# Seven block products for the gate and value projections of a sigmoid-attention and ReGLU kernel

## The chip, the cores and the metric

The kernel runs on one core of a Trainium2 chip. The metric is the device time of one execution in microseconds. The engines of the core work side by side, each through its own queue in order: TensorE (PE; its weight loads are listed apart as PEld), VectorE (DVE), ScalarE (ACT), GpSimd (POOL) and SyncE (SP, which here only issues DMAs). They wait for each other through semaphores.

## The reference

Eight batches of 448 tokens, twelve heads of 64. Sigmoid attention, then a feed-forward layer with a gate; cut to what matters:

```python
scores = np.matmul(q, k.transpose(0, 1, 3, 2)) / np.sqrt(64) - np.log(448)
attn = np.matmul(1.0 / (1.0 + np.exp(-scores)), v)            # 8 x 12 x 448 x 64
x = attn.transpose(0, 2, 1, 3).reshape(3584, 768)
gate = np.maximum(x @ w_gate, 0.0)                            # 3584 x 1536
val = x @ w_val
out = (gate * val) @ w_out                                    # 3584 x 768
```

## The kernel before

**Data.** Everything is cast to 16-bit floats on its way in. The weights `wg`, `wv` and `wo` stay in SBUF. Attention gives x transposed: `xT` is 768 features (six tiles of 128 partitions) by 448 tokens. `hT` is the gated product of two batches ("a group"), 12 feature tiles by 896 tokens.

**The pieces of work on TensorE.** A *score unit* (`qk_unit`, line 292) makes the scores of four heads for one of seven key chunks: four matmuls on quarters of the array that run side by side, into two PSUM banks, from which ACT takes two sigmoids into a tile `PT`. *PV* (`pv`, line 239) multiplies seven such tiles with v for four heads, into two banks, from which DVE scales two tiles of `xT` (`put_xT`, line 174). A *projection* (`gv`, line 304, an "f" below) makes one tile of 128 gate and value features for one batch: six matmuls into one bank for the gate, six into another for the value. ACT takes the relu of the gate (line 318), DVE multiplies it with the value into `hT` (line 327). A *down pair* (`down_pair`, line 413, a "y") makes the output of two token tiles by seven block products in place of eight, with sums of the weights (`weight_sums`, line 385, once) and of the tokens (`token_sums`, line 396) that DVE makes. `down` (line 341) makes the seventh token tile of a group in the plain way.

**Order.** It is written out by hand: engines execute in the order of the program text. The loop at line 562 runs over the batches; a batch has 21 score units in six *bursts* of three or four (`cuts`), PV at the third unit of some bursts (`pv_at`), and after each burst the items that the string `mix[m]` names: "f" takes the next projection from a queue, "y" the next down item. While batch b does its attention, the projections of batch b-1 run. After the loop come the last batch's twelve projections and the last group's down items.

**PSUM.** There are eight banks in two rings of four, given out in turn (`next_ring`, line 71). A projection takes two, a score unit two, PV two. A matmul into a bank waits until the engine that read its last content is done.

**Loads and transposes.** The next batch's q, k and v are loaded from POOL's queue (`load`, `load_v`, lines 98 and 104) after the first burst of a batch, when DVE has copied the present ones out (`dma_transposes`, line 208). SP's queue holds the transposing DMAs that give `qkT` (line 216) and the stores of the output (line 339).

Of the kernel before, what the change touches and what calls it, by code (L numbers as in the profile page):

```python
# [17 lines left out]
def kernel(  # L18
# [36 lines left out]
    xTp = ctx.enter_context(tc.tile_pool(name="xTp", bufs=2 * NPAIR))  # L55
    hTp = ctx.enter_context(tc.tile_pool(name="hTp", bufs=2))
    ysbp = ctx.enter_context(tc.tile_pool(name="ysbp", bufs=4))
    gsbp = ctx.enter_context(tc.tile_pool(name="gsbp", bufs=4))
# [3 lines left out]
    rings = [ctx.enter_context(tc.tile_pool(name="ring0", bufs=4, space=bass.MemoryType.PSUM))]  # L62
# [6 lines left out]
    turn = [0]  # L69

    def next_ring():
        i = turn[0] // 4 % len(rings)
        turn[0] += 1
        return rings[i]

    def bank(name):
        return next_ring().tile([P, 512], FP32, tag="ring", name=name)

    def bank16(name):
        return next_ring().tile([P, 1024], FP16, tag="ring", name=name)  # L80
# [88 lines left out]
    def xT_of(b, pr):  # L169
        if (b, pr) not in xT_tiles:  # L170
            xT_tiles[(b, pr)] = xTp.tile([P, S], FP16, tag="xT", name="xT")
        return xT_tiles[(b, pr)]

    def put_xT(b, pr, q0, qn, src):
        nc.vector.tensor_scalar(  # L175
            out=xT_of(b, pr)[:, q0 : q0 + qn],
            in0=src,
            scalar1=XSCALE,
            scalar2=None,
            op0=AOP.mult,  # L180
        )
# [78 lines left out]
    class FirstSlot:  # L260
# [6 lines left out]
        def unit(self, u):  # L267
# [8 lines left out]
            i = self.number * 4 + u  # L276
            if i % 12 < 2:
                PT = early.tile([P, 2, 512], FP16, tag=f"PT{i % 12}", name="PT")
            else:
                PT = PTp.tile([P, 2, 512], FP16, tag="PT", name="PT")  # L280
# [11 lines left out]
    def qk_unit(b, g, c):  # L292
        ps = [bank("qk_ps") for _ in range(2)]
        qk(qkT_tiles[(b, g)], c, 0, NCH, lambda hh: ps[hh][:, 0:S])
        PT = PTp.tile([P, 2, 512], FP16, tag="PT", name="PT")
        for hh in range(2):
            sigmoid(PT[:, hh, 0:S], ps[hh][:, 0:S])
        PT_tiles[(b, g, c)] = PT

# [4 lines left out]
    def gv(b, q0, qn, f, act_relu):  # L304
        ps = []
        for nm, wt in (("g_ps", wg), ("v_ps", wv)):
            ps.append(bank(nm))
            for dc in range(NDC):
# [3 lines left out]
                    xT_tiles[(b, dc)][:, q0 : q0 + qn],  # L312
# [28 lines left out]
    def down(g, t):  # L341
        last = (g, t) == (B // 2 - 1, 2 * S // P - 1)
        ysb = ysbp.tile([P, DM], FP32, tag="ysb", name="ysb")
        for nm, m0, m1 in (("ya", 0, 512), ("yb", 512, DM)):
# [9 lines left out]
            if m0 == 0 or not last:  # L354
                nc.vector.tensor_scalar(
                    out=ysb[:, m0:m1], in0=ps[:, 0 : m1 - m0], scalar1=OUT_SCALE, scalar2=None, op0=AOP.mult
                )
                if last:
                    store(g, t, ysb, m0, m1, (nc.sync, nc.sync))
            else:  # L360
                nc.scalar.activation(
                    ysb[:, m0:m1], ps[:, 0 : m1 - m0], AF.Copy, scale=OUT_SCALE
                )
        if last:
            store(g, t, ysb, 512, DM, (nc.sync, nc.scalar))
        else:
            store(g, t, ysb, 0, DM, (nc.sync, nc.sync))
# [5 lines left out]
    HF, HM = NFC // 2, DM // 2  # L373
    late = {}

    def open_late():
        first_sbuf.close()
        pool = ctx.enter_context(tc.tile_pool(name="late", bufs=1))
        late["T"] = pool.tile([P, 4, HF, HM], FP16, tag="T", name="T")
        late["pool"] = pool  # L380

    def sub(o, a, b):
        nc.vector.tensor_tensor(out=o, in0=a, in1=b, op=AOP.subtract)
# [10 lines left out]
    sums = {}  # L394

    def token_sums(g, p, pool=None, tag="S"):
        h = hT_tiles[g]
        if pool is None:
            S3 = late["pool"].tile([P, 3, HF * P], FP16, tag="S", name="S")
        else:  # L400
            S3 = pool.tile([P, NPAIR, NCH * D], FP16, tag=tag, name="S")
            S3 = S3[:].rearrange("p x y -> p (x y)")[:, 0 : 3 * HF * P].rearrange("p (i y) -> p i y", i=3)
        S1, S2, S4 = (S3[:, i, :].rearrange("p (f t) -> p f t", f=HF) for i in range(3))
        t1, t2 = (slice(t * P, (t + 1) * P) for t in (2 * p, 2 * p + 1))
        A11, A12 = h[:, 0:HF, t1], h[:, HF:NFC, t1]
        A21, A22 = h[:, 0:HF, t2], h[:, HF:NFC, t2]
# [4 lines left out]
        sums[(g, p)] = S1, S2, S4, A21  # L411

    def down_pair(g, p, then=None):
        h, T = hT_tiles[g], late["T"]
        S1, S2, S4, S3 = sums.pop((g, p))
        t1, t2 = (slice(t * P, (t + 1) * P) for t in (2 * p, 2 * p + 1))
        y1, y2 = (ysbp.tile([P, DM], FP32, tag="ysb", name="ysb") for _ in range(2))
        lo, hi = slice(0, HM), slice(HM, DM)

        def product(ps, A, W, first=True):  # L420
            for f in range(HF):
                nc.tensor.matmul(  # L422
                    ps[:, 0:HM],
                    A[:, f, :],
                    W[:, f, :],
                    start=(first and f == 0),
                    stop=(f == HF - 1),
                    skip_group_check=True,
                )

        def plus(o, ps, u):
            nc.vector.scalar_tensor_tensor(  # L432
                out=o, in0=ps[:, 0:HM], scalar=OUT_SCALE, in1=u, op0=AOP.mult, op1=AOP.add
            )

        a = bank("y11")
        product(a, h[:, 0:HF, t1], wo[:, 0:HF, lo])
        nc.vector.tensor_scalar(
            out=y1[:, lo], in0=a[:, 0:HM], scalar1=OUT_SCALE, scalar2=None, op0=AOP.mult
        )  # L440
        b = bank("u3")
        product(b, S2, T[:, 1])
        plus(y1[:, hi], b, y1[:, lo])
        c = bank("y12")
        product(c, S1, T[:, 0])
        product(b, S3, T[:, 2], False)
        plus(y2[:, lo], b, y1[:, lo])
        plus(y2[:, hi], c, y2[:, lo])
        d = bank("y21")
        product(d, h[:, HF:NFC, t2], T[:, 3])  # L450
        plus(y2[:, lo], d, y2[:, lo])
        store(g, 2 * p + 1, y2, 0, DM, (nc.sync, nc.sync))
        if then is not None:
            then()
        product(a, h[:, HF:NFC, t1], wo[:, HF:NFC, lo], False)
        nc.scalar.activation(y1[:, lo], a[:, 0:HM], AF.Copy, scale=OUT_SCALE)  # L456
        product(c, S4, wo[:, HF:NFC, hi], False)
        plus(y1[:, hi], c, y1[:, hi])
        store(g, 2 * p, y1, 0, DM, (nc.sync, nc.sync))
# [10 lines left out]

    def push_down(g):
        for p in range(3):
            y_queue.append(lambda p=p: down_pair(g, p))
        y_queue.append(lambda: down(g, 6))
# [64 lines left out]
    def pv_finish(b):  # L539
        pv_group(b, NG - 1)  # L540
        push_gv(b, 0, S, range(NFC))
        if b % 2:
            push_down(b // 2)

    first_psum.close()
    rings.insert(0, ctx.enter_context(tc.tile_pool(name="ring1", bufs=4, space=bass.MemoryType.PSUM)))
    turn[0] = 0
# [12 lines left out]

    ffn_mix("f", [(1, lambda: both(1, 0))])
    for b in range(1, B):
        cuts = (0, 3, 6, 9, 13, 17, 21) if b == 1 else (0, 4, 7, 11, 14, 18, 21)
        pv_at = {3: 0, 5: 1} if b == 1 else {0: -1, 2: 0, 4: 1}
# [9 lines left out]
        elif b == 2:  # L574
            mix = ["ff", "ff", "ff", "ff", "ff", "ff"]
# [79 lines left out]
```

## Time and profile before

| | |
|---|---|
| median of 3 runs | 416.93 us (416.25 to 418.12) |
| the profiled execution, its own time | 417.76 us |
| the span in its profile, first to last instruction | 416.0 us |
| granted TensorE clock, mean over the span | 0.998 |
| matmuls of gate and value on 448 tokens | 504 + 504, busy 109.6 + 109.0 us |
| score matmuls, PV matmuls on 448 tokens | 588 and 588, busy 39.8 and 32.2 us |
| sigmoids of 448 columns on ACT | 294, busy 133.2 us |
| relu of the gate on ACT, 448 columns | 84, mean 571 ns |
| products into hT on DVE, 448 columns | 84, mean 620 ns |
| xT from PSUM on DVE, 448 columns | 42, busy 24.3 us |
| DMA issues on POOL | busy 49 us, most of it before 70 us |

In the rows of a profile that follow, a row of the timeline has start and length in microseconds, engine, line, operation, what it writes and reads, how many instructions are merged, and in brackets the idle time before it with what ended it. A row of the chain has start, length and what the end of the program depended on there. A row of the groups has busy time and mean of one in nanoseconds. Matmuls are pipelined: the length of a group of six holds the delay of the last one through the array, so the time from one group's start to the next one's is what TensorE pays.

### The profile page before, as it was taken

The numbers are of one execution on the slowest core, as the hardware profiler recorded it, in microseconds if no ns is written. First come the engines' busy times: TensorE is split into PE (matmuls) and PEld (weight loads), VectorE is DVE, ScalarE is ACT, GpSimd is POOL, SyncE is SP. The second block draws the span as 40 slices with busy tenths as digits, with TensorE's granted clock in tenths as the row PEclk, the third lists the DMA queues.
The fourth block names the chain that finished last, engine by engine and source line by source line (L and its number), as shares of the span: only waits on it lengthen the run. The fifth ranks groups of instructions, "written<-read, shape, count | busy, mean of one in ns | idle before, by whom it ended". The sixth has DMA issues, their size and how long they took to land.

```text
span 416.0 us, 8578 instructions
## 1 busy us (share of the span) xinstructions
PE 406.9 (98%) x3596; PEld 225.9 (54%) x3596; DVE 183.9 (44%) x361; ACT 206.2 (50%) x436; POOL 49.4 (12%) x72
## 2 busy tenths in 40 slices
PE   8999999998999999999999999999999999999996
PEld 3678675554455555555455555454445455455563
DVE  2453344232956554533355443443353442522572
ACT  5856767675653434636564346537553634222100
POOL 8642304300300003000030000300000000000000
PEclk9999999999999999999999999999999999999999
DMA  9999976999883356933289053953431221000054
GB/s 152 198 200 204 204 107 104 202 204 164 105 141 77 81 128 105 185 77 71 44 71 230 21 121 84 149 95 79 88 46 28 50 60 41 16 0 2 14 134 119
DMA packets 68792, 43.68 MB, mean 105 GB/s; under 512 B 35857, under 2 KB 65169, under 8 KB 68753
## 3 DMA queue, kind: packets, MB, share of 16 engines
q0 software_dynamic: 30736, 23.33, 37.5%
q1 hardware_dynamic: 37664, 19.47, 24.4%
q8 instruction: 28, 0.46, 0.5%
q10 hardware_dynamic: 352, 0.33, 0.3%
q14 instruction: 12, 0.09, 0.1%
HBM read 47.19 MB, written 11.01 MB: 140 GB/s over the span
## 4 chain that ended last, share of the span: by engine, by line
PE 85%; DMA 13%; POOL 1%; issue 0%; DVE 0%; ACT 0%; POOLq 0%
PE g_ps L309 24%; PE v_ps L309 23%; PE y L422 14%; PE qk_ps L229 7%; PE pv_ps L247 7%; PE u L422 6%; DMA v<-in_v_dram 4%; DMA wg<-in_moe_w_gate_dram 4%; PE ya L347 2%; DMA qkT<-rel 2%; DMA q<-in_q_dram 2%; DMA k<-in_k_dram 1%; PE yb L347 1%; DVE xT L175 0%; PE trt L198 0%
## 5 line engine op out<-in xcount | busy, mean ns | idle before, releaser
L184 ACT ACTIVATE PT<-qk_ps 128x448 f16<-128x448 f32 (+3 forms) x318 | 151.2, 583 | 54.4 <-PE qk_ps L229 53.2
L309 PE MATMUL g_ps<-xT,wg 128*128 128x448 f16 (+2 forms) x648 | 127.4, 332 | 0.2 <-DVE xT L175 0.2
L309 PE MATMUL v_ps<-xT,wv 128*128 128x448 f16 (+2 forms) x648 | 126.8, 332 | 0.0
L327 DVE TENSOR_TENSOR hT<-gate_sb,v_ps 128x448 f16<-128x448 f32 (+2 forms) x108 | 60.7, 568 | 138.6 <-PE v_ps L309 84.7
L318 ACT ACTIVATE gate_sb<-g_ps 128x448 f32<-128x448 f32 (+2 forms) x102 | 53.9, 541 | 73.6 <-PE g_ps L309 73.4
L309 PEld LDWEIGHTS <-wg 128*128 128x128 f16 x648 | 58.5, 98 | 56.0 <-issue 15.0
L309 PEld LDWEIGHTS <-wv 128*128 128x128 f16 x648 | 62.4, 98 | 47.3 <-issue 0.4
L229 PE MATMUL qk_ps<-qkT 64*64 64x448 f16 (+2 forms) x756 | 47.8, 336 | 2.3 <-DMA qkT<-rel 1.5
L175 DVE TENSOR_SCALAR xT<-pv_ps 128x448 f16<-128x448 f32 (+2 forms) x54 | 28.4, 567 | 31.1 <-PE pv_ps L247 31.0
L456 ACT ACTIVATE ysb<-y 128x384 f32<-128x384 f32 x12 | 5.9, 491 | 70.7 <-PE y L422 70.7
L247 PE MATMUL pv_ps<-PT,v 64*64 64x448 f16 (+2 forms) x756 | 37.5, 329 | 1.2 <-DMA v<-in_v_dram 0.6
L422 PEld LDWEIGHTS <-hT 128*128 128x128 f16 x288 | 28.2, 98 | 19.3 <-issue 0.2
L102 POOL DMA_DIRECT2D k<-in_k_dram x14 | 11.0, 783 | 178.8 <-DVE rel L212 172.1
L229 PEld LDWEIGHTS <-qkT 64*64 64x64 f16 x756 | 18.2, 105 | 23.5 <-issue 14.3
L247 PEld LDWEIGHTS <-v 64*64 64x64 f16 x756 | 21.9, 107 | 12.6 <-issue 1.7
L422 PEld LDWEIGHTS <-S 128*128 128x128 f16 x216 | 21.1, 98 | 14.0
L422 PE MATMUL y<-wo,hT 128*128 128x384 f16 x144 | 27.3, 326 | 0.0
L432 DVE SCALAR_TENSOR_TENSOR ysb<-y,ysb 128x384 f32<-128x384 f32 x36 | 20.1, 557 | 12.7 <-PE y L422 10.7
L432 DVE SCALAR_TENSOR_TENSOR ysb<-u,ysb 128x384 f32<-128x384 f32 x24 | 13.4, 558 | 20.5 <-PE u L422 20.2
L422 PE MATMUL u<-T,S 128*128 128x384 f16 x72 | 13.7, 326 | 0.0
L422 PE MATMUL y<-T,S 128*128 128x384 f16 x72 | 13.7, 326 | 0.0
L422 PE MATMUL y<-T,hT 128*128 128x384 f16 x72 | 13.7, 326 | 0.0
(43 smaller groups left out, 184.8 us busy)
## 6 DMA issues: line engine op xcount, KB each, us to landing
out_dram<-ysb SPq DMA_DIRECT2D x54, 192.0 KB, 2.7
k<-in_k_dram POOLq DMA_DIRECT2D x5, 672.0 KB, 11.2
q<-in_q_dram POOLq DMA_DIRECT2D x5, 672.0 KB, 13.6
v<-in_v_dram POOLq DMA_DIRECT2D x8, 336.0 KB, 15.2
v<-in_v_dram POOLq DMA_DIRECT2D x16, 168.0 KB, 14.8
k<-in_k_dram POOLq DMA_DIRECT2D x8, 224.0 KB, 10.8
wo<-in_moe_w_out_dram POOLq DMA_DIRECT2D x1, 1536.0 KB, 19.6
q<-in_q_dram POOLq DMA_DIRECT2D x6, 224.0 KB, 11.7
```

The costliest lines, as they stand in the source:

```text
L102: nc.gpsimd.dma_start(t16[:, xs, cs], rows_of(src, b)[:, xs, cs])
L175: nc.vector.tensor_scalar(out=xT_of(b, pr)[:, q0 : q0 + qn], in0=src, scalar1=XSCALE, scalar2=None, op0=AOP.mult,)
L184: nc.scalar.activation(PT_ap, ps_ap, AF.Sigmoid, bias=sig_bias, scale=qk_scale)
L229: nc.tensor.matmul(out_of(hh)[o : o + 64, :], qkT[rows, c, cols], qkT[rows, NCH + c0 : NCH + c1, cols], start=True, stop=True, tile_positi ...
L247: nc.tensor.matmul(ps[hh][64 * r : 64 * r + 64, 0:qn], v16[rows, 2 * g + hh, c * D : (c + 1) * D], pieces[c][rows, hh, :], start=(c == 0), ...
L309: nc.tensor.matmul(ps[-1][:, 0:qn], wt[:, dc, f * P : (f + 1) * P], xT_tiles[(b, dc)][:, q0 : q0 + qn], start=(dc == 0), stop=(dc == NDC - 1),
L318: nc.scalar.activation(gate_sb[:, 0:qn], ps[0][:, 0:qn], AF.Relu)
L327: nc.vector.tensor_tensor(out=hT_tiles[g][:, f, o : o + qn], in0=gate_sb[:, 0:qn], in1=ps[1][:, 0:qn], op=AOP.mult,)
L347: nc.tensor.matmul(ps[:, 0 : m1 - m0], hT_tiles[g][:, f, t * P : (t + 1) * P], wo[:, f, m0:m1], start=(f == 0), stop=(f == NFC - 1),)
L422: nc.tensor.matmul(ps[:, 0:HM], A[:, f, :], W[:, f, :], start=(first and f == 0), stop=(f == HF - 1), skip_group_check=True,)
L432: nc.vector.scalar_tensor_tensor(out=o, in0=ps[:, 0:HM], scalar=OUT_SCALE, in1=u, op0=AOP.mult, op1=AOP.add)
L456: nc.scalar.activation(y1[:, lo], a[:, 0:HM], AF.Copy, scale=OUT_SCALE)
```

## The change

For the groups of batches 2 and 3, 4 and 5, 6 and 7, gate and value are made for two feature tiles and both batches at once by `gv_pair` (a "w" item). With the two halves of the 768 features, (wg, wv) is a 2 by 2 block matrix and the two batches' xT another; seven block products of three matmuls each, on sums of blocks, stand in for eight. POOL makes the sums of the weights (`gate_sums` once, in place in `wv`; `unit_sums` for each item, one item ahead), DVE those of the two batches (`batch_sums`). Of the six banks that an item takes, one pair `b` collects four products and is read in between: ACT copies, DVE adds. Batches 0 and 1 keep `gv`.

The down pair is rewritten in the same form, with three banks (`b`, `c`, `a`) in place of four. Banks are given out from a list; `later` moves those in use to its end in the order in which they come free. `xT` is one tile a batch (three buffers), `hT` has one buffer in place of two, `gsb` seven in place of four. Batches 3 to 7 have five bursts of 4, 4, 4, 4 and 5 units in place of six; in the last, PV comes after the first unit. Batch 2 takes ten projections in place of twelve and batch 3 the other two. After each burst from the third of batch 3 on, one item of `work` runs: for a group six "w", the single tile "t", and three "y". Before an item the sums of the next are issued (`prepare`); in a down pair that is done before its seventh product. The last group's w, t and y follow the loop, so that the last work is a down pair.

```diff
-    xTp = ctx.enter_context(tc.tile_pool(name="xTp", bufs=2 * NPAIR))
-    hTp = ctx.enter_context(tc.tile_pool(name="hTp", bufs=2))
+    xTp = ctx.enter_context(tc.tile_pool(name="xTp", bufs=3))
+    hTp = ctx.enter_context(tc.tile_pool(name="hTp", bufs=1))
-    gsbp = ctx.enter_context(tc.tile_pool(name="gsbp", bufs=4))
+    gsbp = ctx.enter_context(tc.tile_pool(name="gsbp", bufs=7))
...
+    def bank(name, shape=(P, 512), dtype=FP32):
+        pool, tag = free[0]
+        free.rotate(-1)
+        return pool.tile(list(shape), dtype, tag=tag, name=name)
+    def later(order):
+        keys = [free[i - 8] for i in order]
+        for key in keys:
+            free.remove(key)
+            free.append(key)
...
+    def gate_sums(f0, f1):
+        fs = slice(f0 * P, f1 * P)
+        sub(wv[:, 0:HD, fs], wg[:, 0:HD, fs], wv[:, 0:HD, fs], nc.gpsimd)
+    def unit_sums(g, f):
+        S1, S2, S4 = sums_tile(2 * P)
+        fs = slice(f * P, (f + 2) * P)
+        A11, A12 = wg[:, 0:HD, fs], wg[:, HD:NDC, fs]
+        S3, A22 = wv[:, 0:HD, fs], wv[:, HD:NDC, fs]
+        sub(S2, A22, S3, nc.gpsimd)
+        nc.gpsimd.tensor_tensor(out=S1, in0=S2, in1=A11, op=AOP.add)
+        sub(S4, A12, S2, nc.gpsimd)
+    def batch_sums(g):
...
+        sub(T1, B12, B11)
+        sub(B12, B22, B12)
+        sub(T2, B22, T1)
+        sub(T4, B21, T2)
+    def gv_pair(g, f):
...
+        b, c, a = ([bank(nm) for _ in range(2)] for nm in ("u", "g2", "g1"))
+        later((6, 7, 4, 5, 2, 3))
+        gs = [[gsbp.tile([P, S], FP32, tag="gsb", name="gsb") for _ in range(3)] for _ in range(2)]
...
+        product(b, 0, B11)
+        copy(0, b)
+        product(c, 3, T1)
+        copy(2, c)
+        product(b, 4, T2, False)
+        copy(1, b)
+        product(a, 1, B21)
+        plus(0, a)
+        product(b, 5, T3, False)
+        plus(2, b)
+        product(c, 6, B22, False)
+        plus(1, c)
+        product(b, 2, T4, False)
+        for u in range(2):
+            gated(u, 0, gs[u][0][:], b[u][:, 0:S])
+        for u in range(2):
+            gated(u, S, gs[u][1][:], gs[u][2][:])
...
-        cuts = (0, 3, 6, 9, 13, 17, 21) if b == 1 else (0, 4, 7, 11, 14, 18, 21)
-        pv_at = {3: 0, 5: 1} if b == 1 else {0: -1, 2: 0, 4: 1}
+        if b == 1:
+            cuts, pv_at = (0, 3, 6, 9, 13, 17, 21), {3: (0, 2), 5: (1, 2)}
+        elif b == 2:
+            cuts, pv_at = (0, 4, 7, 11, 14, 18, 21), {0: (-1, 2), 2: (0, 2), 4: (1, 2)}
+        else:
+            cuts, pv_at = (0, 4, 8, 12, 16, 21), {0: (-1, 2), 2: (0, 2), 4: (1, 1)}
...
-            mix = ["ff", "ff", "ff", "ff", "ff", "ff"]
+            mix = ["ff", "ff", "f", "ff", "f", "ff"]
         elif b == 3:
-            mix = ["fff", "fff", "fy", "fy", "fy", "fy"]
+            mix = ["f", "f", "", "", ""]
             open_late()
...
-            ffn_mix(mix[m], hooks.get(m, ()))
+            if mix[m]:
+                ffn_mix(mix[m], hooks.get(m, ()))
+            elif b > 2:
+                next_work()
     pv_finish(B - 1)
-    last = B // 2 - 1
-    token_sums(last, 0)
-    ffn_mix("f" * NFC)
...
+    push_group(B // 2 - 1)
+    while work:
+        next_work()
```

The helpers of `gv_pair`: `product` runs one block product for both feature tiles (two times three matmuls of 448 columns), `copy` is two ACT copies out of PSUM, `plus` two DVE additions of PSUM onto such a copy, `gated` a DVE operation max(gate, 0) x value into `hT`; for the second batch both its inputs lie in SBUF. The new down pair runs, in this order, a product into `b`, one into `c`, one onto `b`, one into `a`, one onto `b`, one onto `c` and one onto `b`, each read by DVE or ACT before the next onto the same bank. DMAs stay as many, except that the last output tile's store is issued in four parts instead of two, and two of the last stores come from ACT's queue.

## The prediction

> **What bounds the kernel now.** I read the page first (engine shares, the chain that ended last), then the chain in order of time, then the timeline of one burst in the middle and of the start of batch 3.
>
> ```profile
> PE 406.9 (98%) x3596; PEld 225.9 (54%) x3596; DVE 183.9 (44%) x361; ACT 206.2 (50%) x436; POOL 49.4 (12%) x72
> PE 85%; DMA 13%; POOL 1%; issue 0%; DVE 0%; ACT 0%; POOLq 0%
> ```
>
> The chain is TensorE for 85% of the span; its DMA part lies at the start and at one place near 92 us. From 104 us on TensorE never waits more than some tenths. So an item's cost is its matmuls' issue time, read from the chain: six of 448 columns 1.136 us (a "product" below), 24 of 384 columns 3.90.
>
> ```profile
> 363.82 1.14 PE v_ps L309 x6
> 364.96 1.14 PE g_ps L309 x6
> 391.56 3.90 PE y L422 x24
> ```
>
> One burst of the present kernel: two score units, PV, two units, then projections.
>
> ```profile
> 206.82 0.57 PE L229 MATMUL qk_ps<-qkT 64*64 64x448 f16 x8
> 207.22 1.49 PE L247 MATMUL pv_ps<-PT,v 64*64 64x448 f16 x28
> 207.25 3.60 ACT L184 ACTIVATE PT<-qk_ps 128x448 f16<-128x448 f32 x8 [0.91 <-PE qk_ps L229]
> 208.75 1.16 DVE L175 TENSOR_SCALAR xT<-pv_ps 128x448 f16<-128x448 f32 x2 [1.13 <-PE pv_ps L247]
> 209.03 1.31 PE L309 MATMUL g_ps<-xT,wg 128*128 128x448 f16 x6
> 210.66 0.62 ACT L318 ACTIVATE gate_sb<-g_ps 128x448 f32<-128x448 f32 x1
> ```
>
> Two units take 0.40 us of TensorE, PV 1.33. The first sigmoid starts 0.43 after the first score matmul; eight take 3.41 until ACT starts its next operation (207.25 to 210.66), 0.43 each. The relu of g_ps is thus 0.4 us late here already, and nobody minds: the next projection has other banks.
>
> The start of batch 3:
>
> ```profile
> 92.37 9.96 DMA qkT<-rel
> 102.38 0.57 PE L229 MATMUL qk_ps<-qkT 64*64 64x448 f16 x8 [1.50 <-DMA qkT<-rel]
> 105.98 0.55 DVE L383 TENSOR_TENSOR T<-wo 128x768 f16<-128x768 f16 x1
> 109.98 1.14 DVE L327 TENSOR_TENSOR hT<-gate_sb,v_ps 128x448 f16<-128x448 f32 x2
> ```
>
> TensorE waits 1.5 us for the transposed q and k, and eight weight sums hold DVE from 105.98 to 109.98, while the products of the first projection are left in PSUM.
>
> **The change part by part. Removed.** Gate and value for a feature tile of two batches take 7 products of 3 matmuls instead of 8: 756 matmuls for 864, 108 fewer at 0.1893 us: -20.4. Bursts of batches 3 to 7 fall from 30 to 25. A change from projections to scores and back costs 0.32 (212.44 + 1.136 = 213.58 to the next g_ps at 214.37 is 0.79, less 0.57 for three units, plus the first product's 1.24 for 1.14): -1.6. The down products keep their 42 matmuls a pair. Together -22.0.
>
> **Batch 3 starts no earlier.** Batch 2 gives two projections (4.54) to batch 3, so TensorE is ready at 100.8 - 4.5 = 96.3. The transpose is issued one projection earlier (90.1), but it landed only when the loads of k, q, wo and v, issued by 76.9 as before, had drained: DMA still moves 205 GB/s in 94:96. If it lands at 102.3 as now, the wait grows by 4.5; if landing follows its issue, by 2.3. I take 4.5, since the loads do not move.
>
> **Weight sums uncovered.** Three projections followed them in the first burst of batch 3, now one. Its multiply still comes behind eight sums, 7.6 us after the batch's start, and ends at 8.2. The fourth score unit of the next burst needs that bank and is ready at 5.2: +3.1 (2 to 4).
>
> **Two banks for three products.** The pair item holds six banks; its third product adds onto the first, so it waits for two ACT copies of it, and these stand behind the burst's sigmoids. In a burst without PV: copies start at 0.43 + 3.41 = 3.84, the first ends at 4.44 (0.60 as the relu), product 3 can start at 4.5. TensorE has spent 0.8 on units, 0.13 on the change, 1.24 and 1.14 on two products: 3.3. Wait 1.2. Where a pair came just before, the fourth unit also waits 0.25 for the bank of its last gate, which comes off the 1.2. Six such bursts (batches 4 to 7): +7.2. With PV ahead the 1.33 us cover it; without that cover these too would cost 1.2. The bound is 0 (copies slip in) to 1.7 (a further ACT latency): 0 to 10.
>
> **Five units in the last burst.** PV now comes after the first unit, so unit five takes PV's two banks. xT copies start 1.76 after the burst's start, the second ends at 2.9; the unit was due at 2.1: +0.85 in five batches. In the two with a pair item, ten sigmoids let product 3 start at 6.04 for 5.67: +0.4 each. Together +5.0 (3 to 6).
>
> **Moved or re-cut at nothing.** ACT gets six copies for four relus, DVE ten operations for four: 14 x 0.43 = 6.0 and about 6.5 us of a cycle of 10, covered. One hT buffer: the next group is written only after TensorE has read the last pair. POOL queues pair sums behind next batch's k, q, v issues (3.7 us); they are due a whole item later, 8 to 10 us. SP has transposes behind the stores of at most one pair, 2.8 us for four, two bursts ahead of need. The end: three issues at 0.55 on SP and an ACT issue ahead of the last copy, less the 0.2 that xT cost at 361: +0.6.
>
> **POOL beside DVE.** Each pair item brings three POOL operations on 768 elements, which no row shows. DVE's own take 0.55; POOL's one-input select takes 0.288 for 128 elements, 0.1 of it fixed: 1.2 for 768, double for two inputs 2.4. Three stay under 7.95 us even so.
>
> ```profile
> L383 DVE TENSOR_TENSOR S<-hT,S 128x768 f16<-128x768 f16 x12 | 6.7, 558 | 0.4
> masks.py:199 POOL TENSOR_SCALAR_AFFINE_SELECT ident<-ident 128x128 f16<-128x128 f16 x1 | 0.3, 288 | 0.1
> ```
>
> What they do to DVE operations that run beside them is open. From below nothing: the T sums at 106 to 110 took 0.55 us with POOL issuing DMAs and without. From above each waits out the other (1.2 us a time) wherever DVE reads SBUF twice. POOL starts when product 6 has freed the sums' slot, so its three operations run over product 7 and the burst after it. Then the gates out of SBUF, ready 0.67 us into the burst, take turns with POOL and end at 3.8 instead of 1.7. Behind them in DVE's order stands xT: product 2 starts 1.0 later in four bursts with PV, and unit five 2.1 later in two last bursts, of which 0.4 only replaces the wait for copies: 4 x 1.0 + 2 x 1.7 = 7.4. The four batch sums take turns too, and the one for product 3 ends 6.5 us after the last pair's sixth product instead of 3.1; the final group's product 3 comes 3.3 late, those of two groups inside the batches, already 1.2 late, 1.0: 5.3. In the tail seven copy buffers serve six copies a pair, and the copy that waits for the late gate holds product 5 by 0.5, five times: 2.5. Together 15. No row is near to a computing POOL, so I take the middle, 7.6, and keep 0 and 15.
>
> [...]
>
> **Sum**, on the profiled execution (417.76; its span 416.0): -22.0 + 4.5 + 3.1 + 7.2 + 5.0 + 0.6 = -1.6, so 416.2; with 7.6 it is 423.8. The median of the runs (416.93) lies 0.83 below the profiled execution: 423.0.
>
> **Rivals.** (1) Forecast: the saved matmuls come back as waits, and POOL and DVE hinder each other: 419 to 430, 423 the middle. (2) The waits come, but POOL costs DVE nothing: 416.9 - 1.6 = 415.3. For it: T sums undisturbed by POOL's issues. Against it: these compute nothing. (3) Not slower: ACT's copies are not the last to arrive. It decides at product 3: if the copies are done by 3.3 us into the burst, the 7.2 and 0.4 x 2 vanish; with POOL harmless and only the batch 3 terms (7.6) and 0.85 x 5 left, 416.9 - 22.0 + 7.6 + 4.2 + 0.6 = 407.3; if those are hidden too, 396. For it: ACT is half idle (50%). Against it: the relu above started 3.84 after the burst's start, in order. (4) POOL sets the pace: three operations over 7.95 us, 2.65 each, which is just above my 2.4. At 3.3 the six tail items cost 2 us more each, 12, on top of the full 15: 416.9 - 1.6 + 15 + 12 = 442. That the matmuls are not saved is excluded: the built program holds 108 fewer.
>
> **How the numbers follow.** 0.5% (2.1 us; 414.8 to 419.0) is what can be told from no change. Case 1 has 0.52, case 2 0.20, case 3 0.22, case 4 0.06. Slower: 0.52 + 0.06 = 0.58. Case 2 straddles the lower bound: 0.14 same, 0.06 faster. Faster 0.28. The forecast's own range is 419 to 430; leaving out half of case 3, most of case 4 and a little of case 1, the range is 406 to 433.
>
> **What would show it.** Right: TensorE waiting for ACT's copy at the third product in bursts without PV (about 1 us), for DVE's xT at unit five, about 6 us for qkT at the start of batch 3, and DVE gates or batch sums well over 0.55 us when POOL computes. Wrong: pair items back to back at 7.95 us inside the batches; POOL operations under 0.8 us; a first wait in batch 3 under 4 us.

## The result, and the profile after

The changed kernel takes 451.51 us (median of 4 runs, 449.93 to 452.77); the kernel before, run beside it, 417.01 (416.25 to 418.12). The ratio is 1.082, 95% interval 1.077 to 1.087. The forecast was 423.0, its range 406 to 433: the direction is right, the size is not.

From the page of the changed kernel, the engines' busy time, the clock granted to TensorE in 40 slices, and the chain that ended last:

```profile
PE 400.8 (89%) x3488; PEld 220.8 (49%) x3488; DVE 289.8 (65%) x470; ACT 226.9 (51%) x483; POOL 160.9 (36%) x132
...
PEclk9999999997589999989999999999999988999999
...
PE 52%; DVE 21%; DMA 14%; issue 7%; ACT 3%; POOL 2%; ACTq 0%; DVEq 0%; POOLq 0%
```

The 108 matmuls are gone (3488 for 3596), but TensorE is busy for 89% of the span where it was 98%. DVE had 0% of the chain before and has 21% now. From 100 us to the end TensorE is not busy for 41.3 us; in the kernel before it was 5.6.

Who TensorE waited for (the view of waits: total in us, number, longest):

```profile
PE qk_ps L234 <- DVE hT L329: 11.8, 1, 11.8
PE qk_ps L234 <- DMA qkT<-rel: 6.6, 1, 6.6
PE u L387 <- DVE X L378: 6.2, 3, 3.1
PE u L387 <- DVE ysb L434: 4.2, 3, 3.6
PE u L387 <- ACT gsb L523: 4.1, 4, 1.0
PE qk_ps L234 <- DVE xT L180: 4.0, 7, 1.6
```

The second, fifth and sixth rows are waits that the prediction named, near the sizes it gave. The first is one wait of 11.8 us where it had 3.1. The third lies at the batch sums, which its POOL term held; the fourth, most of it, at token sums, which it did not. The first wait in the timeline (start, length, engine, line, operation):

```profile
109.81 0.55 DVE L378 TENSOR_TENSOR T<-wo 128x768 f16<-128x768 f16 x1
...
110.40 9.58 DVE L378 TENSOR_TENSOR T<-wo,T 128x768 f16<-128x768 f16 x1
111.57 7.99 POOL L378 TENSOR_TENSOR wv<-wg,wv 128x768 f16<-128x768 f16 x5
119.90 0.55 DVE L378 TENSOR_TENSOR T<-wo 128x768 f16<-128x768 f16 x1
...
120.84 0.61 DVE L329 TENSOR_TENSOR hT<-gate_sb,v_ps 128x448 f16<-128x448 f32 x1
...
121.50 0.58 PE L234 MATMUL qk_ps<-qkT 64*64 64x448 f16 x3 [11.77 <-DVE hT L329]
122.02 2.42 PE L311 MATMUL g_ps<-xT,wg 128*128 128x448 f16 x6
```

One weight sum, 0.55 us for its neighbours, took 9.58: POOL ran five gate sums through it, and the sum ended 0.4 us after POOL's last. (It starts 1.2 us ahead of POOL's first; POOL's spans in the profile are rough.) The multiply behind it (120.84) held the bank that TensorE wanted. The next six matmuls then took 2.42 us instead of 1.31, at half the clock (granted 0.50 from 121.4 to 126 us; the 5 in the clock row above). The same in small, all over the second half (groups by shape: busy us, mean ns):

```profile
L532 DVE SCALAR_TENSOR_TENSOR hT<-gsb 128x448 f16<-128x448 f32 x36 | 38.5, 1110 | 0.0
...
L532 DVE SCALAR_TENSOR_TENSOR hT<-gsb,u 128x448 f16<-128x448 f32 x36 | 20.6, 614 | 0.0
...
L378 DVE TENSOR_TENSOR X<-xT,X 128x1344 f16<-128x1344 f16 x6 | 12.1, 2012 | 0.1
L217 DVE COPY rel<-k 128x896 f16<-128x896 f16 x18 | 10.9, 606 | 0.0
```

The gates whose operands both lie in SBUF take 1.11 us; the same operation with one operand in PSUM takes 0.61. The batch sums take 2.01, and a plain copy inside SBUF 0.61 for the 0.38 of before. A last burst shows what follows:

```profile
192.34 1.49 PE L252 MATMUL pv_ps<-PT,v 64*64 64x448 f16 x28
...
192.78 2.60 DVE L532 SCALAR_TENSOR_TENSOR hT<-gsb 128x448 f16<-128x448 f32 x2
192.87 2.02 POOL L484 TENSOR_TENSOR S<-S,wg 128x768 f16<-128x768 f16 x1
194.85 2.02 POOL L378 TENSOR_TENSOR S<-wg,S 128x768 f16<-128x768 f16 x1
...
195.30 1.14 DVE L180 TENSOR_SCALAR xT<-pv_ps 128x448 f16<-128x448 f32 x2
195.96 0.35 PE L234 MATMUL qk_ps<-qkT 64*64 64x448 f16 x1 [1.55 <-DVE xT L180]
...
198.13 2.45 PE L387 MATMUL g<-X,S 128*128 128x448 f16 x6
```

Of the two gates the second is held by POOL until 195.4 (2.06 us for it alone). xT starts after them, and the fifth unit waits for xT's banks: its first matmul comes 1.9 us after the one before, 0.5 in a kernel without sums on POOL (e1 below). Two microseconds later a product runs at half clock (2.45 us for 1.31; granted 0.50 from 198.1 to 200.6 us).

### The profile page after: what moved, and what is told of

It is laid out like the page before. It is cut to its first block, busy times and chain, and to the rows that moved or that the text cites. A ratio compares the mean times of both kernels' runs of the same rounds, so it can differ in the third digit from the quotient of the medians.

```text
span 448.7 us, 8763 instructions
## 1 busy us (share of the span) xinstructions
PE 400.8 (89%) x3488; PEld 220.8 (49%) x3488; DVE 289.8 (65%) x470; ACT 226.9 (51%) x483; POOL 160.9 (36%) x132
## 4 chain that ended last, share of the span: by engine, by line
PE 52%; DVE 21%; DMA 14%; issue 7%; ACT 3%; POOL 2%; ACTq 0%; DVEq 0%; POOLq 0%
PE u L387 21%; PE g L387 10%; PE y L387 7%; DMA v<-in_v_dram 7%; DVE hT L532 5%; PE qk_ps L234 4%; PE pv_ps L252 4%; DVE gsb L527 3%; DMA k<-in_k_dram 3%; DVE X L378 3%; DMA qkT<-rel 3%; DVE T L378 3%; PE ya L348 2%; ACT PT L189 2%; DVE xT L180 2%
## 5 line engine op out<-in xcount | busy, mean ns | idle before, releaser
L387 PEld LDWEIGHTS <-S 128*128 128x128 f16 x540 | 53.2, 99 | 64.3 <-issue 15.8
L234 PE MATMUL qk_ps<-qkT 64*64 64x448 f16 (+2 forms) x756 | 51.4, 339 | 23.6 <-DVE hT L329 11.8
L527 DVE TENSOR_TENSOR gsb<-g,gsb 128x448 f32<-128x448 f32 x72 | 42.9, 624 | 37.8 <-PE g L387 37.8
L523 ACT COPY gsb<-u 128x448 f32<-128x448 f32 x72 | 38.4, 582 | 29.3 <-PE u L387 28.3
L180 DVE TENSOR_SCALAR xT<-pv_ps 128x448 f16<-128x448 f32 (+2 forms) x54 | 28.3, 566 | 21.4 <-PE pv_ps L252 20.7
L532 DVE SCALAR_TENSOR_TENSOR hT<-gsb 128x448 f16<-128x448 f32 x36 | 38.5, 1110 | 0.0
L484 POOL TENSOR_TENSOR S<-S,wg 128x768 f16<-128x768 f16 x18 | 36.2, 2008 | 1.4
L378 POOL TENSOR_TENSOR S<-wg,S 128x768 f16<-128x768 f16 x18 | 35.8, 1988 | 0.0
L311 PE MATMUL g_ps<-xT,wg 128*128 128x256 f16 (+2 forms) x216 | 34.6, 297 | 0.1
L311 PE MATMUL v_ps<-xT,wv 128*128 128x256 f16 (+2 forms) x216 | 34.2, 295 | 0.0
L387 PEld LDWEIGHTS <-wv 128*128 128x128 f16 x216 | 21.3, 99 | 20.3 <-issue 0.9
L387 PEld LDWEIGHTS <-wg 128*128 128x128 f16 x216 | 20.6, 99 | 21.3 <-issue 4.2
```

The source lines that it names most:

```text
L180: nc.vector.tensor_scalar(out=xT_tiles[b][:, pr, q0 : q0 + qn], in0=src, scalar1=XSCALE, scalar2=None, op0=AOP.mult,)
L234: nc.tensor.matmul(out_of(hh)[o : o + 64, :], qkT[rows, c, cols], qkT[rows, NCH + c0 : NCH + c1, cols], start=True, stop=True, tile_positi ...
L311: nc.tensor.matmul(ps[-1][:, 0:qn], wt[:, dc, f * P : (f + 1) * P], xT_tiles[b][:, dc, q0 : q0 + qn], start=(dc == 0), stop=(dc == NDC - 1),)
L378: eng.tensor_tensor(out=o, in0=a, in1=b, op=AOP.subtract)
L387: nc.tensor.matmul(ps[:, 0:n], A[:, k_, :], W[:, k_, :], start=(first and k_ == 0), stop=(k_ == kn - 1), skip_group_check=True,)
L484: nc.gpsimd.tensor_tensor(out=S1, in0=S2, in1=A11, op=AOP.add)
```

## Experiments

The question was what makes the 28.5 us between forecast and result: POOL beside DVE, or the new waits for banks, copies and bursts. Each run was timed beside the kernel before (medians 416.9 to 417.3). Since qkT of batch 3 lands between 100.3 and 103.9 us from run to run, comparisons below also use the time from the first score of batch 3 to the end of the profiled span: 313.6 us before, 345.8 in the changed kernel.

**e1, all sums on DVE.**

```diff
-        sub(wv[:, 0:HD, fs], wg[:, 0:HD, fs], wv[:, 0:HD, fs], nc.gpsimd)
+        sub(wv[:, 0:HD, fs], wg[:, 0:HD, fs], wv[:, 0:HD, fs])
...
-        sub(S2, A22, S3, nc.gpsimd)
-        nc.gpsimd.tensor_tensor(out=S1, in0=S2, in1=A11, op=AOP.add)
-        sub(S4, A12, S2, nc.gpsimd)
+        sub(S2, A22, S3)
+        nc.vector.tensor_tensor(out=S1, in0=S2, in1=A11, op=AOP.add)
+        sub(S4, A12, S2)
```

> The 6 gate sums and 54 unit sums are issued on DVE instead of POOL, nothing else. Theory (POOL's computing holds DVE, and that is what my sum mis-sized): the 12.1 us stall in batch 3, the 3.7 us one at 358, the batch sums of 1.7 to 3.3 us and the late unit five go; the structural waits of the prediction (4.5 + 3.1 + 7.2 + 5.0 + 0.6 against 22.0 saved) stay: 417 us, between 412 and 423; DVE sums 0.55 us each, gates out of SBUF near 0.6 instead of 1.11. Rival (the new waits are those of banks, copies and bursts, and POOL is beside the point): above 440 us, the same stalls at the same places. Second rival (DVE has no room for 60 more sums, 33 us): 430 to 440, with TensorE waiting for gates behind the sums in every pair item.

Measured: 430.8 us (429.3 to 433.1), ratio 1.033 (1.028 to 1.037), 20.7 less than the changed kernel (18.4 from batch 3's start, in the profiled executions). The rival that POOL is beside the point is out. But 417 was missed by 14. The gates out of SBUF are back to the time of the others, and the waits that are left are these:

```profile
PE qk_ps L234 <- DMA qkT<-rel: 7.7, 1, 7.7
PE u L387 <- ACT gsb L523: 4.8, 6, 1.0
PE g L387 <- ACT PT L189: 3.5, 2, 1.8
PE g L387 <- DVE S L484: 2.9, 1, 2.9
PE qk_ps L234 <- DVE hT L329: 2.8, 1, 2.8
PE qk_ps L234 <- DVE ysb L355: 1.7, 1, 1.7
```

```profile
L532 DVE SCALAR_TENSOR_TENSOR hT<-gsb 128x448 f16<-128x448 f32 x36 | 20.8, 618 | 0.0
```

Rows 3, 4 and 6 are e1's own. The first unit's sums stand behind the batch sums in DVE's order and hold the second product (at 159.30, put down to a sigmoid that had long ended: DVE's second unit sum ended at 159.24); the gate sums stand ahead of a down item's copies. Counted as gaps of TensorE these are 3.8, 3.1 and 1.9 us, and behind the last one 1.7 us are lost at half clock (granted 0.86 over 120 to 130 us and 0.97 over the next ten): 10.5. Without them e1 would stand near 420.3. That is a subtraction, and no run shows it; by it POOL's price in the changed kernel lies between some 20 and 31 us.

**e2, only the gate sums on DVE** (the first line of e1's diff).

> Only the 6 gate sums of batch 3 move to DVE; the 54 unit sums stay on POOL. Theory (the one weight sum of 9.58 us was held by five POOL sums in a row): the 12.1 us stall falls to the 2 to 4 of the prediction and the half clock behind it with it: 451.5 - 9 - 2 = 440 us, between 437 and 444, all 12 weight sums at 0.55. Rival (that stall is the uncovered first multiply behind eight weight sums, whoever sits beside it): 449 to 452, stall of 10 us or more at the same place.

Measured: 442.7 us (439.4 to 445.3), 8.8 less than the changed kernel. All weight sums take 0.55, and of the long wait this is left:

```profile
PE qk_ps L234 <- DVE hT L329: 2.0, 1, 2.0
```

So all but 2 of the 11.8 us were POOL's, and the uncovered multiply by itself is 2.0 here and 2.8 in e1, as forecast (2 to 4). It was not POOL's issuing of DMAs: the sum that took 9.58 us above takes 0.56 here (at 110.41), beside the same issues. The unit sums account for the other 11.9 between e2 and e1.

**e3 and e4, the kernel before with POOL made to compute.** Nobody uses the results. They stand behind POOL's loads in batch 3, beside weight and token sums of DVE. In e3 all ten write one tile:

```diff
+                if b == 3:
+                    scratch = late["pool"].tile([P, 5, P], FP16, tag="scratch", name="scratch")
+                    for _ in range(10):
+                        nc.gpsimd.tensor_tensor(
+                            out=scratch[:], in0=wg[:, 0:5, 0:P], in1=wv[:, 0:5, 0:P], op=AOP.subtract
+                        )
```

> The kernel before, with ten POOL subtractions of 640 fp16 elements (results unused) behind POOL's loads in batch 3, so that they run from about 110 to 124 us, beside four weight sums and four token sums of DVE at 112.2. Theory (a DVE operation with both inputs in SBUF is held for a whole run of POOL operations): one DVE sum of 8 to 12 us instead of 0.55, the rest at 0.55, a TensorE stall of 5 to 10 us and 423 to 428 us in all. Rival 1 (they take turns, one POOL operation each): eight DVE sums of 1.5 to 2.2 us, none above 3; 420 to 427. Rival 2 (no interference): 417, all sums at 0.55.

Measured: 427.5 us (427.2 to 427.8), ratio 1.025 (1.023 to 1.026). The time suits my theory and lies just above rival 1's, but the trace is rival 1's: ten sums of 1.6 to 1.8 us, none longer. They took turns.

```profile
108.76 14.85 POOL L618 TENSOR_TENSOR scratch<-wg,wv 128x640 f16<-128x640 f16 x9
...
110.80 1.74 DVE L383 TENSOR_TENSOR T<-wo,T 128x768 f16<-128x768 f16 x1
...
112.46 1.67 DVE L327 TENSOR_TENSOR hT<-gate_sb,v_ps 128x448 f16<-128x448 f32 x3
...
114.06 1.62 DVE L383 TENSOR_TENSOR T<-wo 128x768 f16<-128x768 f16 x1
```

Each sum waits for one POOL operation and goes between it and the next; three multiplies with an operand in PSUM pass unhindered at 0.55 each. What differs from the changed kernel? There the five gate sums write different slices and carry no wait. In e3 every operation waits on a semaphore of the one before, since all write one tile (the trace's records have these waits). Hence e4, six sums into different slices, the first four with no wait between them:

```diff
+                if b == 3:
+                    for _ in range(3):
+                        scratch = ysbp.tile([P, 2, HF, P], FP16, tag="ysb", name="scratch")
+                        for k_ in range(2):
+                            nc.gpsimd.tensor_tensor(
+                                out=scratch[:, k_], in0=wg[:, 0:HF, 0:P], in1=wv[:, 0:HF, 0:P], op=AOP.subtract
+                            )
```

> Like e3, but six POOL subtractions of 768 elements into slices of three free output buffers, so that the first four have no semaphore between them (in e3 all ten wrote one tile and each waited on the one before; in the changed kernel the five gate sums in a row have no waits either). Theory (POOL gives the memory port up only where it waits between two operations): POOL's run goes at its own 1.64 us each, one DVE sum is held 6 us or more, the others take 0.55; 421 to 426 us. Rival (they take turns operation by operation, and the 9.58 us were something else): as in e3, POOL near 2.0 each, DVE sums 1.6 to 2.0 each and none above 3; 420 to 425.

Measured: 429.4 us (428.8 to 429.9), ratio 1.030 (1.028 to 1.032), above my 421 to 426, but with the trace that the theory asks for:

```profile
108.73 11.19 DVE L383 TENSOR_TENSOR T<-wo,T 128x768 f16<-128x768 f16 x1
109.91 9.59 POOL L619 TENSOR_TENSOR scratch<-wg,wv 128x768 f16<-128x768 f16 x6
119.84 0.55 DVE L383 TENSOR_TENSOR T<-wo 128x768 f16<-128x768 f16 x1
...
121.44 1.12 PE L229 MATMUL qk_ps<-qkT 64*64 64x448 f16 x7 [9.22 <-DVE hT L327]
```

POOL goes at its own 1.60 a sum, one DVE sum is held for all of it (the one wait among the six, for a semaphore that is not POOL's and was long satisfied, gave no turn), and TensorE stalls 9.2 us: the picture of 110 us in the changed kernel, made in the old one. The "memory port" of the theories of e4 and e8 is my supposition: the runs show which operation was held and for how long, not what held it.

**e8, the opposite in the changed kernel:** a tiny POOL copy behind each gate sum, which waits for it.

```diff
         sub(wv[:, 0:HD, fs], wg[:, 0:HD, fs], wv[:, 0:HD, fs], nc.gpsimd)
+        nc.gpsimd.tensor_copy(gate[0:1, :], wv[0:1, 0, fs][:, 0:2])
```

> The changed kernel with a tiny POOL copy of two elements behind each of the six gate sums, which waits for that sum; nothing else. Theory (POOL keeps the memory port through operations that follow each other with no semaphore wait, and gives it up at a wait): no DVE weight sum above 3 us; the three that are left at 110 us take 1.6 to 2.0 each, the multiply behind them ends near 115.5 instead of 121.5, the 12.1 us stall falls to 6 to 8: 451.5 - 5 = 446 us, between 443 and 449. Rival (POOL's amount of work decides, whether it waits or not): one weight sum of 8 us or more, 450 to 453.

Measured: 446.2 us (446.0 to 447.7), 5.3 less with more work on POOL.

```profile
110.73 1.65 POOL L378 TENSOR_TENSOR wv<-wg,wv 128x768 f16<-128x768 f16 x1
112.44 0.40 POOL L477 COPY gate<-wv 1x2 f16<-1x2 f16 x1
112.72 2.12 DVE L378 TENSOR_TENSOR T<-wo 128x768 f16<-128x768 f16 x1
...
114.49 0.39 POOL L477 COPY gate<-wv 1x2 f16<-1x2 f16 x1
114.76 2.12 DVE L378 TENSOR_TENSOR T<-wo,T 128x768 f16<-128x768 f16 x1
```

DVE now gets one sum through at each of POOL's waits. One sum still took 3.25 us (I had said none above 3), and the stall, counted as the 12.1 was, is 8.4 where I had 6 to 8.

This is not the whole rule. Of a pair item's three POOL sums the second waits for the first, but the third waits for nothing. By the theory a DVE operation would be held through both. In the changed kernel DVE got through between the second and the third all the same, in all 15 places where one of its operations was waiting: in the last burst shown above POOL's sums run from 192.87 and from 194.85, and the held gate ends at 195.4, 0.5 us behind the second's end and 1.5 ahead of the third's. In the two runs that let nobody in (e4 and the five gate sums) no operation had waited for POOL's own work from the run's start on, and both stand straight behind DMA issues. Which of the two matters is open.

**e5, the order of a pair's products** (on e1): the fourth goes second.

```diff
         product(b, 0, B11)
         copy(0, b)
+        product(a, 1, B21)
+        plus(0, a)
         product(c, 3, T1)
         copy(2, c)
         product(b, 4, T2, False)
         copy(1, b)
-        product(a, 1, B21)
-        plus(0, a)
```

> e1 (430.8 us) with the products of a pair item in the order 1, 4, 2, 3, 5, 6, 7: the second is now the one that needs neither a sum nor a copied bank. Theory (the third product waits for ACT's two copies, which stand behind eight sigmoids, and in the first item of a group the second waits for sums): the four waits of 1.19, two of 0.53, two of 1.91 and most of one of 3.1 us go: 420 us, between 417 and 423. Rival (ACT is simply late, and the fourth product takes the wait over): 427 to 431.

Measured: 427.3 us (425.6 to 428.8); from batch 3's start 324.2 for e1's 327.4. The waits for ACT's copies of 1.19 us are gone, so their cause was right. The size was missed by 7. The second product now waits 0.6 for its bank in six bursts, and the fifth, which follows the fourth on the same bank, waits 0.22 for a copy in all 18 items: some 7.5 us that I had not seen coming.

**e6, bursts of 5, 4, 4, 4, 4 units** (on e1), no fifth unit behind a PV.

```diff
-            cuts, pv_at = (0, 4, 8, 12, 16, 21), {0: (-1, 2), 2: (0, 2), 4: (1, 1)}
+            cuts, pv_at = (0, 5, 9, 13, 17, 21), {0: (-1, 3), 2: (0, 1), 3: (1, 4)}
...
+            if m in pv_at and pv_at[m][1] == cuts[m + 1] - cuts[m]:
+                pv_group(b, pv_at[m][0])
```

> e1 (430.8 us) with batches 3 to 7 cut into bursts of 5, 4, 4, 4, 4 units, PV behind the third unit, behind the first of the third burst and at the end of the fourth burst, so that no fifth unit follows a PV. Theory (unit five waits for the two banks that PV has just taken): five times 1.0 us and 0.3 of half clock behind it go: 424 us, between 422 and 427. Rival (ACT's sigmoids hold the burst anyway): 429 to 432, the wait at another unit or at PV.

Measured: 435.0 us (431.7 to 436.1), from batch 3's start 329.8: slower. No unit waits for xT any more, but PV at a burst's end waits for its last sigmoids, and eight pairs for ACT's copies instead of six. The rival's waits came, but the time is above its 429 to 432 too. I read it so that ACT's sigmoids are still to come, whichever instruction meets them; what made it slower than e1 is not shown.

**e7, dummy matmuls in the wait for qkT** (on e1).

```diff
+                if b == 2 and m == count - 1:
+                    keep_warm(36)
```

> e1 (430.8 us) with 36 matmuls whose result nobody reads (6.8 us) at the end of batch 2, where TensorE waits 7.9 us for qkT. Theory (the scores and PV after that wait run at half clock because TensorE had been idle, which my sum left out): batch 3's first burst at full clock, 428 us, between 427 and 429.5. Rival (the half clock there is not from idling): 430 to 432.

Measured: 431.3 us, but from 428.7 to 434.6, so the medians decide nothing. The one profiled run took 324.4 us from batch 3's start to the end for e1's 327.4. Its timeline, from the dummies to the first PV:

```profile
95.64 6.97 PE L175 MATMUL warm_ps<-zeros 128*128 128x448 f16 x36
...
102.95 1.49 PE L252 MATMUL pv_ps<-PT,v 64*64 64x448 f16 x28
```

That PV took 1.49 us; it is 2.54 in e1 and 2.46 in the changed kernel. From the first score to the first projection it is 2.2 us for 3.6 in e1, so the lower clock behind the idling (granted 0.66 over 100 to 110 us in e1) costs that burst 1.4 us. The other 1.6 of the 3.0 lie behind the wait for the weight sums: it is 2.75 us in both, but e1 runs at half clock after it (113.6 to 117.0; granted 0.83 over 110 to 120 us) and e7 does not (five matmuls of 448 columns in 1.12 us at 111.13). The mean granted clock of e7's runs goes with their times: 0.996 at 428.7 us, 0.992 at 430.9 and 431.6, 0.984 at 434.6. Why it differs between runs stays open.

**e9 to e12, a version without the named costs.** e9 has all sums on DVE and the first units' sums an item ahead; batch 2 keeps 12 projections; batch 3 has four bursts, its weight sums behind the first down item; where ACT's copies are late the fourth product goes ahead of the third. The core of it:

```diff
-            mix = ["ff", "ff", "f", "ff", "f", "ff"]
+            mix = ["ff"] * 6
...
+        elif b == 3:
+            cuts, pv_at = (0, 6, 11, 16, 21), {0: (-1, 3), 1: (0, 4), 3: (1, 1)}
...
+                next_work("cab" if m not in pv_at or m == 4 else "cba")
+                if b == 3 and m == 0:
+                    weight_sums(0, HF)
```

> The seven products kept, each cost that the runs showed taken away: all sums on DVE, the gate sums spread over the first group's unit sums and the first units' sums made an item ahead; batch 2 keeps its 12 projections, batch 3 has four bursts and its weight sums behind its first down item; in bursts without PV, and where it is the last, product 4 goes ahead of product 3; the fifth unit's wait is left. Theory (the terms add up): from the start of batch 3 (102.4 us) e1 needed 327.4 us; less 4.5 (two projections moved under the loads), 2.9 (half clock), 3.6 (weight sums), 2.7 (gate sums on DVE), 4.2 (copies) and 6.9 (sums late in the first item of a group) is 302.6, with the 1.7 around the span 406.7 us, between 403 and 413. Rival (a wait removed is only passed on, as in e6): 416 to 426.

Measured: 415.5 us (414.6 to 418.0), ratio 0.9975 (0.9957 to 0.9993), about the time of the kernel before: 9 short of the sum of its terms. The longest waits left were late sums again:

```profile
PE u L387 <- DVE ysb L434: 2.7, 3, 2.0
PE g L387 <- DVE X L378: 1.9, 2, 1.2
```

e10 moves them, and product 6 ahead of product 5:

```diff
+                if b == 3 and m == 0:
+                    weight_sums(0, HF, (0,))
...
+                    weight_sums(0, HF, (1, 2))
...
         elif groups < B // 2:
             unit_sums(groups, 0)
+            first_batch_sum(groups)
```

> e9 (415.5 us) with its four largest late sums and copies moved: the weight sums split (first before the down item, two behind it, the last behind the first down pair's third product), the first batch sum made an item ahead (it needs only the first half of the second batch's xT), and product 6 ahead of product 5 where product 4 is ahead of product 3. Theory (these waits hide nothing else): 2.2 + 2.2 + 4 x 0.35 off, and some half clock behind them: 409.5 us, between 407.5 and 412. Rival (passed on to the next wait, as most of e9's gain was): 414 to 416.

Measured: 413.4 us (412.9 to 414.0), ratio 0.991 (0.990 to 0.993). That misses the 407.5 to 412. The two rows are nearly gone, but the seventh product now waits for DVE's sum of the fifth nine times, 4.2 us in gaps: passed on in part. e11 adds a PT buffer and sets PV behind the second unit of the last burst. A shorter tile of zeros makes room for the buffer, so the warm-up matmuls at the program's start are shorter and more:

```diff
-    PTp = ctx.enter_context(tc.tile_pool(name="PTp", bufs=10))
+    PTp = ctx.enter_context(tc.tile_pool(name="PTp", bufs=11))
...
-            cuts, pv_at = (0, 4, 8, 12, 16, 21), {0: (-1, 2), 2: (0, 2), 4: (1, 1)}
+            cuts, pv_at = (0, 4, 8, 12, 16, 21), {0: (-1, 2), 2: (0, 2), 4: (1, 2)}
```

> e10 with an eleventh PT buffer (made room for by a shorter tile of zeros for the warm-up matmuls), so that PV of the last burst of batches 4 to 7 comes behind the second unit and the fifth unit takes no bank of PV. Theory (unit five waits for PV's banks): 4 x 0.8 off e10: 3 us less, between 1.5 and 4.5. Rival (as in e6, ACT's ten sigmoids of 4.3 us hold the burst, and the projection's first bank takes the wait over): within 1 us of e10.

Measured: 410.5 us (409.7 to 410.6), ratio 0.984 (0.982 to 0.985), 2.9 less than e10 as expected (2.3 from batch 3's start on). This version takes 1.6% less than the kernel before and 9% less than the changed one. Whether its eleventh PT buffer would help the kernel before too was not run. TensorE is busy for 96% of the span, and no slice has a lower clock:

```profile
PE 393.3 (96%) x3521; PEld 221.4 (54%) x3521; DVE 272.6 (67%) x522; ACT 225.7 (55%) x483; POOL 49.4 (12%) x72
...
PEclk9999999999999999999999999999999999999999
```

e12 is e11 with the 60 sums back on POOL, the reverse of e1's diff.

> e11 (410.5 us) with the gate and unit sums back on POOL, everything else as in e11. Theory (sums on POOL cost what they do to DVE, wherever they stand): as between e1 and e2, where the unit sums alone cost 12 us: 421 us, between 417 and 426, gates out of SBUF near 1.1 us again. Rival (made an item ahead and with 31 us less for DVE to do, POOL's sums are hidden): 407 to 411.

Measured: 434.5 us (432.6 to 435.4), ratio 1.042 (1.040 to 1.044): 24.1 more than e11, and above the 426 that I had allowed. Where some of it goes is seen ahead of the first group:

```profile
134.12 1.94 POOL L378 TENSOR_TENSOR wv<-wg,wv 128x768 f16<-128x768 f16 x1
134.49 1.98 DVE L378 TENSOR_TENSOR hT<-hT 128x768 f16<-128x768 f16 x1
136.40 1.14 DVE L180 TENSOR_SCALAR xT<-pv_ps 128x448 f16<-128x448 f32 x2
137.06 1.12 PE L234 MATMUL qk_ps<-qkT 64*64 64x448 f16 x4 [5.42 <-DVE xT L180]
```

xT itself is not held (its source is PSUM; 1.14 us for two, as in the kernel before, 1.15 to 1.16), but four token sums ahead of it took turns with POOL, the last of them beside a sum of POOL that had no wait. A unit waits 5.4 us for the bank. Making POOL's sums early does not help: it is the other engine that pays.

## Why the prediction was wrong

**The step that failed is "POOL beside DVE",** a term of the sum that was mis-sized: 7.6 us taken, 15 kept as the upper end. Measured are 20.7 by e1, at most 31 if e1's own waits are taken off, and 24.1 between e11 and e12. By place, in the gaps of the changed kernel, it is about 27. Four things were wrong in it.
- The places were incomplete, and that is most of it. The gate sums were not set against the weight sums of the same burst, which were costed as a step of their own: 9 us. Nor were the token sums and xT ahead of the last group: 3.7 us of waiting at 358. Half clock behind the longer waits (at 198, 358 and 372; granted 0.50, 0.50 and 0.60 in the 2.5 to 4 us from there) took another 4.8.
- The middle between 0 and 15 had no row behind it. At the places that it did list, the 15 came out as 9.6: product 2 lost 2.0 for 4.0, unit five 2.8 for 3.4, the batch sums 4.8 for 5.3 (3.3 of it at the final group's third product, as forecast), and the tail's copies nothing for 2.5.
- "Each waits out the other (1.2 us a time)" assumes turns, operation by operation. The unit sums did take turns. The gate sums did not: one DVE sum waited for all five, 9.6 us.
- One POOL sum takes 1.64 us, and 2.0 when DVE comes between. The 1.2 was stretched from a select on 128 elements, with one input, though the same paragraph puts two inputs at 2.4. The 0.1 us taken as fixed in it is what POOL's MEMSETs of one column took in the kernel before (0.10); that a second input doubles the time was an estimate that no run shows.

On who is held, the trace agrees with the upper end, DVE operations that read SBUF twice: gates out of SBUF took 1.11 us (0.62 in e1), gates with a PSUM operand 0.61 (0.61 in e1). On how long, it does so only in part: at the unit sums a hold lasted over one POOL operation, but at the gate sums over five (9.58 us) and in e4 over six (11.19 us).

Every sign that the prediction named for being right came: the copies at about 1 us, xT at unit five, some 6 us for qkT, gates and batch sums well over 0.55. They showed that these waits exist and said nothing of the places that were not listed.

**Point by point.**
- Removed, 22.0: the 20.4 are right. 108 matmuls are gone, and the tail's pair items run back to back (378.24 to 386.18, 7.94 us; 7.95 forecast). No run shows the 1.6 for fewer bursts by itself.
- Batch 3 starts no earlier, 4.5: right in kind. Scores began at 102.89 (102.38 before), the wait grew from 1.5 to 6.6. Left out was the lower clock behind it (granted 0.56 from 102.8 to 106 us), 1.3 us here (3.5 us from the first score to the first projection for 2.2) and 1.4 in e1.
- Weight sums uncovered, 3.1: right where POOL keeps away, waits of 2.8 in e1 and 2.0 in e2.
- Two banks for three products, six waits of 1.2: four gaps of 1.19 us are there; in the other two bursts the batch sums' 1.7 us came in their place. e5 confirms the cause.
- Five units in the last burst, 5.0: e1 has 0.65 us five times where 0.85 was put, and 0.53 twice at copies where 0.4 was put: 4.3. Beside a computing POOL the five are 6.0 instead of 3.2, in the changed kernel.
- Costed at nothing: mostly rightly, but not for the first product of a pair item or down pair, which waits for a sigmoid in nine bursts: it starts 0.31 to 0.48 us after the last score for the usual 0.28, 1.0 us in all.
- The end, 0.6: two gaps of 0.45 in the last down pairs.

**Without POOL** the recorded sum was 415.3; e1 less its own waits is 420.3. Of the missing 5 us, e1's profiled execution (433.1 us) shows 3.0 of lower clock behind the waits for qkT and the weight sums, 1.7 more of waiting for qkT than the 4.5, and the 1.0 just named; against these stand 2.4 less at the copies and 0.7 less in the last bursts. That explains about half, and the rest stays open. By this subtraction the structure alone makes this change slightly slower, and POOL makes it far slower. The rival "POOL sets the pace" was not it either: POOL took 1.6 to 2.3 us an operation, not 2.65, and TensorE waited for DVE, not for POOL.

## What to carry to other kernels

Work moved to POOL is not free because POOL is idle: look at which DVE operations read and write SBUF alone while it computes, and price each at one whole POOL operation (1.6 to 2.3 us here). Where POOL's run starts straight behind DMA issues and none of its operations waits for POOL's own work, price one of them at the whole run (9.6 and 11.2 us here). A term for two engines meeting must go through every place where they meet, by the clock of the trace, not only through the steps that the change names. And removing a wait on a path with three others behind it gives less than its size (e6, e9, e10): sum the slack behind it first.

## What the runs showed of the hardware

- How long POOL holds a DVE operation depends on more than the one instruction: 1.6 to 1.75 us a DVE sum when every POOL operation waits for the one before (e3), one of 11.19 when none waits for POOL's own work (e4), one POOL operation at a time in the unit sums, of which the third has no wait (a gate of 2.06 us at 193.3 in the changed kernel). Why DVE got through ahead of the third unit sum and not among the gate sums, no run shows.
- Held in the changed kernel were operations with both operands in SBUF (gates 1110 ns for 618 in e1, batch sums 2012 for 854) and also the copy of k within SBUF, which has one (606 ns in the mean for 383 before). Operations with a PSUM operand were not (gates 614 ns, in e1 614).
- POOL's issuing of DMAs held nobody: in the kernel before, the weight sums that started from 105.98 to 109.51 took 0.55 us, while it issued from 106.06 to 109.73.
- TensorE fell to half speed in the first burst of batch 3 after waits for qkT of 6.2 to 7.7 us (e5, e6, the changed kernel, e1: PV 2.46 to 2.83 us for 1.49), and in the changed kernel also about 2 us after a fifth unit's gaps of 1.9 + 0.5 us (from 198.13 on 0.37 us from one matmul of 448 columns to the next for 0.19; granted clock 0.50). After the 1.7 us at its batch sums it did not (granted 1.00 from 164.9 to 172 us). The length of a wait does not decide by itself: after 2.75 us at the weight sums e1 ran at half clock for 3.4 us, e7 at full clock.
